# Grouping the 64-row matmul pairs of two FFN blocks, moving attention work, and reordering the head of a linear-attention + GeGLU kernel

## Chip, cores, metric

The kernel runs on one core of one Trainium2 chip. The metric is device time in microseconds (us): the median of several executions. "Span" is the time from the first to the last instruction of one profiled execution; it is about 1.7 us shorter than the time of the same execution.

## The reference

A block with two parallel branches on the same normalised input, B=1, S=2048, D=576, 32 heads of 18, F=4608, bf16:

```python
x  = A_x
xn = layernorm(x)
# A: linear attention.  phi(t) = where(t > 0, t + 1, exp(t)) + 1e-6
q, k, v = split_heads(xn @ wqkv)
kv = phi(k).T @ v ; z = sum_s phi(k)            # per head
o  = (phi(q) @ kv) / (phi(q) @ z + 1e-6)
# B: GeGLU
ffn = (gelu(xn @ w_gate) * (xn @ w_up)) @ w_down
return x + o @ wo + ffn
```

## The kernel before

The contraction length 576 is 4 x 128 + 64. The last 64 rows of `w_gate` and of `w_up` are put together in one 128-row tile `wr`, and the last 64 columns of xn are written twice (rows 0-63 and 64-127 of `xnT[:, 4]`). So the two short matmuls, one for gate and one for up, sit in different halves of the array and run at the same time; they are called a *pair* below. The kernel has this order:

1. Head. Per tile of 128 tokens: layernorm (statistics on VectorE, `rstd` on ScalarE), five transposes on TensorE, a copy of the result to `xnT` on VectorE, then K and V projections (20 matmuls of 288 columns). The kv sums accumulate two tiles behind.
2. Query projections.
3. Four chunks of 512 tokens. Each has a gate/up stage (36 column blocks of 128 features) and a down stage (4 tiles x 2 halves, 41 matmuls each).

```python
    load_x(0, 1)
    load_x(1, 1)
    load_wqkv_main(D, 2 * D)                                   # K
    nc.sync.dma_start(wqkv_sb[0:64, 4, :], A_wqkv[512:576, :]) # last 64 rows
    load_x(2, 2)                                               # a pair of x tiles
    load_wqkv_main(2 * D, 3 * D)                               # V
    load_wqkv_main(0, D)                                       # Q
    load_x(4, 4)
    ...
    def layernorm_transpose(n):
        ...
        for a_ in range(2):
            nc.vector.bn_stats(out=stats[:, a_, :], in_=xr[:, a_, :])
        ...                                                    # mv, rstd, xn
        for kt in range(KT):
            nc.tensor.transpose(tp[:, kt, :], xn[:, kt * P:(kt + 1) * P], ident[:])
        nc.vector.tensor_copy(out=xnT[:, :, n * P:(n + 1) * P], in_=tp[:, 0:KT, :])
    ...
    def gu_batch(sc, f0, r):
        wg, wu, wr, blk_dma = load_gu_block(f0, r)
        ...                                                    # 2r PSUM banks: g[i], u[i]
        for i in range(r):                                     # 8r matmuls, 128 rows
            for (pst, wsb) in ((g[i], wg), (u[i], wu)):
                for kt in range(4):
                    nc.tensor.matmul(pst[:], lhsT=wsb[:, kt, fcol], rhs=xnT[:, kt, cs], start=(kt == 0), stop=False)
        for i in range(r):                                     # r pairs, 64 rows
            nc.tensor.matmul(g[i][:], lhsT=wr[0:64, fcol], rhs=xnT[0:64, 4, cs], start=False, stop=True)
            nc.tensor.matmul(u[i][:], lhsT=wr[64:128, fcol], rhs=xnT[64:128, 4, cs], start=False, stop=True)
        for i in range(r):
            ...                                                # gelu on ScalarE, product on VectorE
    for sc in range(NSC):
        if sc == 0:
            for k in range(NF // 2):
                blk_dma = gu_batch(0, 2 * k, 2)
                if k >= NWBUF: load_wd_slice(after=blk_dma)
                if k < NS: attn_num(k)                         # attention of one tile
                if 1 <= k <= NS: attn_T(k - 1)
        else:
            for k in range(NF // RMAX):
                gu_batch(sc, RMAX * k, RMAX)                   # RMAX = 3
        for j in range(TPC):
            ...                                                # down projections
```

The order in which the instructions stand on each engine is not the order of this text: a scheduler decides it at build time from the dependencies and from a model of how long things take.

Of the kernel before, what the change touches and what calls it, by code (L numbers as in the profile page):

```python
# [8 lines left out]
ACT = mybir.ActivationFunctionType  # L9
ALU = mybir.AluOpType  # L10
BF16 = mybir.dt.bfloat16
F32 = mybir.dt.float32
PSUM = bass.MemoryType.PSUM

P = 128
S = 2048
D = 576
# [4 lines left out]
NS = S // P  # L22
NF = F // P
SC = 512
NSC = S // SC
TPC = SC // P
HALF = D // 2
DX = D + 64
KT = 5
# [7 lines left out]
EPS_ATT = 1e-6  # L37
RMAX = 3
NWBUF = 3
WDS = 2  # L40
NWARM = 36
KV_SKEW = 2

# [3 lines left out]
class _Ring:  # L47
    def __init__(self, tiles):
        self.tiles = tiles
        self.i = 0  # L50
# [8 lines left out]
def kernel(  # L59
# [12 lines left out]
    nc = tc.nc  # L72
# [3 lines left out]
    out_view = out_flat.rearrange("(n p) d -> p n d", p=P)  # L76
# [10 lines left out]
    def bank(name, *_):  # L87
        return psum.tile([P, 512], F32, name=name, tag="ps")
# [24 lines left out]
    def load_gu_block(f0, r):  # L113
        c0, c1 = f0 * P, (f0 + r) * P
        w = r * P
        wg = wg_bufs.next()
        wu = wu_bufs.next()
        wr = wr_bufs.next()
        nc.sync.dma_start(wg[:, :, :w], B_w_gate[0:512, c0:c1].rearrange("(kt p) c -> p kt c", p=P))
        nc.sync.dma_start(wu[:, :, :w], B_w_up[0:512, c0:c1].rearrange("(kt p) c -> p kt c", p=P))  # L120
        nc.sync.dma_start(wr[0:64, :w], B_w_gate[512:576, c0:c1])
        last = nc.sync.dma_start(wr[64:128, :w], B_w_up[512:576, c0:c1])
        return wg, wu, wr, last
# [9 lines left out]

    def load_x(n0, cnt):
        if cnt == 1:
            t = awork.tile([P, D], BF16, name="xs", tag="xs", bufs=2)
            nc.sync.dma_start(t[:], x_view[:, n0, :])
            x_src[n0] = t[:]
        else:
            t = awork.tile([P, 4, D], BF16, name="xg", tag="xg", bufs=2)  # L140
            nc.sync.dma_start(t[:, :cnt, :], x_view[:, n0:n0 + cnt, :])
            for i in range(cnt):
                x_src[n0 + i] = t[:, i, :]
# [4 lines left out]
    def load_wqkv_main(c0, c1):  # L148
        nc.sync.dma_start(wqkv_sb[:, 0:4, c0:c1], A_wqkv[0:512, c0:c1].rearrange("(kt p) c -> p kt c", p=P))

    load_x(0, 1)
    load_x(1, 1)
    load_wqkv_main(D, 2 * D)
    nc.sync.dma_start(wqkv_sb[0:64, 4, :], A_wqkv[512:576, :])
    load_x(2, 2)
    load_wqkv_main(2 * D, 3 * D)
    load_wqkv_main(0, D)
    load_x(4, 4)
    X_LATER = {3: (8, 4), 7: (12, 4)}

    bmask = const.tile([P, 7, DA], F32, name="bmask")
# [35 lines left out]
    def phi(ps_ap, out_ap, rows, cols, add_eng):  # L197
# [6 lines left out]
        )  # L204
        add_eng.tensor_tensor(out=out_ap, in0=e[:rows, :cols], in1=a[:rows, :cols], op=ALU.add)  # L205

    def layernorm_transpose(n):
        xt = x_src.pop(n)
        stats = asmall.tile([P, 2, nc.vector.BN_STATS_DIM], F32, name="stats")
        xr = xt.rearrange("p (a b) -> p a b", a=2)  # L210
        for a_ in range(2):
            nc.vector.bn_stats(out=stats[:, a_, :], in_=xr[:, a_, :])
        mv = asmall.tile([P, nc.vector.BN_AGGR_DIM], F32, name="mv")
        nc.vector.bn_aggr(out=mv[:], in_=stats[:])
        rstd = asmall.tile([P, 1], F32, name="rstd")
        nc.scalar.activation(out=rstd[:], in_=mv[:, 1:2], func=ACT.Ln, bias=eps_ln[:], scale=1.0)
        nc.scalar.activation(out=rstd[:], in_=rstd[:], func=ACT.Exp, scale=-0.5)
        xn = awork.tile([P, DX], BF16, name="xn")
        nc.vector.tensor_scalar(
            out=xn[:, 0:D], in0=xt, scalar1=mv[:, 0:1], scalar2=rstd[:],  # L220
            op0=ALU.subtract, op1=ALU.mult,
        )
        nc.vector.tensor_scalar(
            out=xn[:, D:DX], in0=xt[:, 512:D], scalar1=mv[:, 0:1], scalar2=rstd[:],
            op0=ALU.subtract, op1=ALU.mult,
        )
        tp = bank_bf16("tp_x", "tp", 1)
        for kt in range(KT):
            nc.tensor.transpose(tp[:, kt, :], xn[:, kt * P:(kt + 1) * P], ident[:])  # L229
        nc.vector.tensor_copy(out=xnT[:, :, n * P:(n + 1) * P], in_=tp[:, 0:KT, :])  # L230

    def kv_project(n):
        ts_ = slice(n * P, (n + 1) * P)
# [77 lines left out]
    def load_wd_slice(after=None):  # L311
        f0 = wd_loaded[0]
        if f0 < NF:
            d = nc.sync.dma_start(wd_sb[:, f0:f0 + WDS, :], wd_view[:, f0:f0 + WDS, :])
            if after is not None:
                tc.add_manual_dep(
                    d.ins, after.ins.name,
                    mybir.DependencyInfo(mybir.DependencyClass.NoSync, mybir.DependencyReason.DATA),
                    reason="w_down slice after the prefetched gate/up block on the same DMA queue",
                )  # L320
            wd_loaded[0] += WDS

# [27 lines left out]
    def attn_T(n):  # L350
        ts_ = slice(n * P, (n + 1) * P)
        o_sb = o_tiles.pop(n)
        tp = bank_bf16("tp_o")
        for kt, (r0, rn) in enumerate(OB):
            nc.tensor.transpose(tp[:rn, kt, :], o_sb[:, r0:r0 + rn], ident[:])  # L355
        nc.scalar.copy(out=oT[:, 0:3, ts_], in_=tp[:, 0:3, :])
        nc.scalar.copy(out=oT[:96, 3:5, ts_], in_=tp[:96, 3:5, :])

    def gu_batch(sc, f0, r):
        cs = slice(sc * SC, (sc + 1) * SC)  # L360
        wg, wu, wr, blk_dma = load_gu_block(f0, r)
        g = []
        u = []
        for i in range(r):
            g.append(bank("g"))
            u.append(bank("u"))
        for i in range(r):
            fcol = slice(i * P, (i + 1) * P)
            for (pst, wsb) in ((g[i], wg), (u[i], wu)):
                for kt in range(4):  # L370
                    nc.tensor.matmul(  # L371
                        pst[:], lhsT=wsb[:, kt, fcol], rhs=xnT[:, kt, cs],
                        start=(kt == 0), stop=False,
                    )
        for i in range(r):
            fcol = slice(i * P, (i + 1) * P)
            nc.tensor.matmul(g[i][:], lhsT=wr[0:64, fcol], rhs=xnT[0:64, 4, cs], start=False, stop=True)  # L377
            nc.tensor.matmul(u[i][:], lhsT=wr[64:128, fcol], rhs=xnT[64:128, 4, cs], start=False, stop=True)  # L378
        for i in range(r):
            gl = fwork.tile([P, SC], F32, name="gl")  # L380
            nc.scalar.activation(out=gl[:], in_=g[i][:], func=ACT.Gelu_apprx_tanh)  # L381
            nc.vector.tensor_tensor(out=hT[:, f0 + i, :], in0=u[i][:], in1=gl[:], op=ALU.mult)  # L382
        return blk_dma

    for sc in range(NSC):
        if sc == 0:
            nb = NF // 2
            for k in range(nb):
                blk_dma = gu_batch(0, 2 * k, 2)
                if k >= NWBUF:  # L390
                    load_wd_slice(after=blk_dma)
                if k < NS:
                    attn_num(k)
                if 1 <= k <= NS:
                    attn_T(k - 1)
            assert not o_tiles
            while wd_loaded[0] < NF:
                load_wd_slice()
        else:
            for k in range(NF // RMAX):  # L400
                gu_batch(sc, RMAX * k, RMAX)

        for j in range(TPC):
            n = sc * TPC + j
            ts_ = slice(n * P, (n + 1) * P)
            xres = fwork.tile([P, D], BF16, name="xres")
            nc.sync.dma_start(xres[:], x_view[:, n, :])
            res = fwork.tile([P, D], BF16, name="res")
            for hf in range(2):
                a_ps = bank("acc")  # L410
                for f in range(NF):
                    nc.tensor.matmul(  # L412
                        a_ps[:, :HALF], lhsT=hT[:, f, j * P:(j + 1) * P],
                        rhs=wd_sb[:, f, hf * HALF:(hf + 1) * HALF],
                        start=(f == 0), stop=False,
                    )
                for kt, (r0, rn) in enumerate(OB):
                    nc.tensor.matmul(  # L418
                        a_ps[:, :HALF], lhsT=oT[:rn, kt, ts_],
                        rhs=wo_sb[:rn, kt, hf * HALF:(hf + 1) * HALF],  # L420
                        start=False, stop=(kt == KT - 1),
                    )
                nc.vector.tensor_tensor(  # L423
                    out=res[:, hf * HALF:(hf + 1) * HALF], in0=a_ps[:, :HALF],
                    in1=xres[:, hf * HALF:(hf + 1) * HALF], op=ALU.add,
                )
            nc.sync.dma_start(out_view[:, n, :], res[:])


# [28 lines left out]
```

## Time and profile before

| | |
|---|---|
| time | 549.08 us, median of 6 runs (548.30 to 549.86) |
| profiled execution | 548.3 us, span 546.6 us |
| TensorE busy | 98% |
| first K matmul / query projections start | 11.07 / 60.61 us |
| gate/up of chunk 0, its down stage | 82.69, 40.22 us |
| gate/up of chunk 1, its down stage | 72.47, 40.22 us |

The rows with stages are differences between the first matmuls of the stages in the trace. These are lines of the page of the kernel before: busy time, the busy tenths of TensorE in 40 slices, the granted TensorE clock in the same slices, and the chain that ended last.

```profile
PE 535.4 (98%) x3495; PEld 313.7 (57%) x3528; DVE 193.6 (35%) x433; ACT 152.9 (28%) x346; POOL 44.6 (8%) x59
...
PE   5999999999999999999999999999999999999997
...
PEclk8999999999999999999999999999999999999999
...
PE 96%; DMA 1%; DVE 1%; issue 1%; SPq 0%; POOL 0%; ACT 0%; POOLq 0%; ACTq 0%
```

Only the first slice stands out. The Trainium skill ("Perfetto Trace Analysis", Identifying the Most-Contended Engine) warns that matmul busy time does not tell how near the engine is to its limit, because matmuls are pipelined. So look at starts, not at busy time. The timeline of TensorE over the head (start us, length us, engine, line, operation, count, idle before and what ended it):

```profile
5.57 1.27 PE L229 MATMUL tp_x<-ident,xn 128*128 128x128 bf16 x10
...
11.07 2.58 PE L239 MATMUL ps_k<-wqkv_sb,xnT 128*128 128x288 bf16 x10 [4.23 <-DVE xnT L230]
...
13.44 1.74 PE L248 MATMUL ps_v<-wqkv_sb,xnT 128*128 128x288 bf16 x10
...
15.02 0.44 PE L229 MATMUL tp_x<-ident,xn 128*128 128x128 bf16 x5
...
15.29 1.39 PE L239 MATMUL ps_k<-wqkv_sb,xnT 128*128 128x288 bf16 x10
```

The transposes of tiles 0 and 1 are done at 6.84 us, yet the first projection starts at 11.07: it waits for the copy of the transposed tile on VectorE. Ten K matmuls then take 2.58 us where the next tile's ten take 1.39. VectorE's timeline says why the copy was late:

```profile
8.09 1.18 DVE L212 BATCH_NORM_STATS2 stats<-xg 128x6 f32<-128x288 bf16 x3 [1.98 <-DMA xg<-in_A_x_dram]
...
10.53 0.88 DVE L230 COPY xnT<-tp_x 128x640 bf16<-128x640 bf16 x2
```

The statistics of x tiles 2 and 3 stand ahead of the copies of tiles 0 and 1 in VectorE's queue, and they waited for their load. The granted clock (the share of TensorE's full clock that it is given; 1.00 is full) fell in the gap (windows view, 11 to 15 us; after the five busy columns stand the granted clock, here 0.61, the DMA share and GB/s):

```profile
11.00:15.00 4.00, 3.93 (x20) 2.64 (x21) 3.01 (x11) 2.10 (x6) 1.06 (x2) 0.61 1.12 334
```

Inside a gate/up stage, the timeline of TensorE at the end of one block of three (last four 128-row matmuls, pairs, and the first four of the next block):

```profile
209.44 1.03 PE L371 MATMUL u<-xnT,wu 128*128 128x512 bf16 x4
210.40 0.39 PE L377 MATMUL g<-xnT,wr 64*128 64x512 bf16 x1
210.40 0.39 PE L378 MATMUL u<-xnT,wr 64*128 64x512 bf16 x1
...
210.84 0.38 PE L377 MATMUL g<-xnT,wr 64*128 64x512 bf16 x1
...
211.15 1.04 PE L371 MATMUL g<-xnT,wg 128*128 128x512 bf16 x4
```

Four matmuls of 512 columns at 216 ns each, start to start, should give way after 0.86 us; the first pair starts 0.96 us after 209.44. The last pair starts at 210.84 and the next 128-row matmul 0.31 us later, not 0.22. Each change of array mode (from 128-row to 64-row matmuls or back) loses almost 0.1 us, and no view calls TensorE's matmul side idle there. The side that loads weights (PEld) does show something; this is the start of another group of pairs:

```profile
222.47 0.09 PEld L377 LDWEIGHTS <-wr 64*128 64x128 bf16 x1 [0.42 <-issue]
```

The first weight load of the new mode starts 0.01 us before its matmul (222.48), where inside a mode it starts some 0.2 us ahead, and such a load takes 0.09 us, about what a change loses.

### The profile page before, as it was taken

The numbers are of one execution on the slowest core, as the hardware profiler recorded it, in microseconds if no ns is written. First come the engines' busy times: TensorE is split into PE (matmuls) and PEld (weight loads), VectorE is DVE, ScalarE is ACT, GpSimd is POOL, SyncE is SP. The second block draws the span as 40 slices with busy tenths as digits, with TensorE's granted clock in tenths as the row PEclk, the third lists the DMA queues.
The fourth block names the chain that finished last, engine by engine and source line by source line (L and its number), as shares of the span: only waits on it lengthen the run. The fifth ranks groups of instructions, "written<-read, shape, count | busy, mean of one in ns | idle before, by whom it ended". The sixth has DMA issues, their size and how long they took to land.

```text
span 546.6 us, 8832 instructions
## 1 busy us (share of the span) xinstructions
PE 535.4 (98%) x3495; PEld 313.7 (57%) x3528; DVE 193.6 (35%) x433; ACT 152.9 (28%) x346; POOL 44.6 (8%) x59
## 2 busy tenths in 40 slices
PE   5999999999999999999999999999999999999997
PEld 4888664444447774443467754444577644444775
DVE  6995597555541102322321112332301032233101
ACT  3887796333330002222310012322200022232000
POOL 1455463000000000000000000000000000000000
PEclk8999999999999999999999999999999999999999
DMA  9800004966762004544521024554401154440000
GB/s 282 248 2 2 1 2 122 271 194 194 193 199 82 27 23 124 158 131 135 169 87 43 23 88 132 160 164 130 131 23 42 41 169 140 131 130 1 23 12 22
DMA packets 79625, 58.08 MB, mean 106 GB/s; under 512 B 4448, under 2 KB 79520, under 8 KB 79584
## 3 DMA queue, kind: packets, MB, share of 16 engines
q1 hardware_dynamic: 79584, 57.53, 35.7%
q8 instruction: 27, 0.44, 0.3%
q14 instruction: 14, 0.11, 0.1%
HBM read 55.15 MB, written 2.36 MB: 105 GB/s over the span
## 4 chain that ended last, share of the span: by engine, by line
PE 96%; DMA 1%; DVE 1%; issue 1%; SPq 0%; POOL 0%; ACT 0%; POOLq 0%; ACTq 0%
PE acc L412 26%; PE g L371 23%; PE u L371 23%; PE g L377 7%; PE ps_q L294 4%; PE ps_k L239 4%; PE acc L418 4%; PE ps_v L248 3%; PE po L333 1%; DMA xg<-in_A_x_dram 1%; PE tp_o L355 1%; PE kv_ps L191 1%; PE tp_x L229 1%; DMA wr<-in_B_w_up_dram 0%; POOL pk L205 0%
## 5 line engine op out<-in xcount | busy, mean ns | idle before, releaser
L381 ACT ACTIVATE gl<-g 128x512 f32<-128x512 f32 x144 | 76.2, 596 | 330.4 <-PE u L378 330.3
L382 DVE TENSOR_TENSOR hT<-u,gl 128x512 bf16<-128x512 f32 x144 | 91.1, 684 | 190.6 <-ACT gl L381 190.6
L371 PE MATMUL u<-xnT,wu 128*128 128x512 bf16 x567 | 147.3, 379 | 0.8
L412 PE MATMUL acc<-wd_sb,hT 128*128 128x288 bf16 x1152 | 146.4, 286 | 0.0
L371 PE MATMUL g<-xnT,wg 128*128 128x512 bf16 x552 | 144.8, 380 | 1.0
L412 PEld LDWEIGHTS <-hT 128*128 128x128 bf16 x1152 | 112.2, 98 | 30.2 <-issue 1.7
L371 PEld LDWEIGHTS <-wu 128*128 128x128 bf16 x576 | 56.3, 98 | 68.0
L371 PEld LDWEIGHTS <-wg 128*128 128x128 bf16 x576 | 52.9, 98 | 69.7 <-issue 14.0
L423 DVE TENSOR_TENSOR res<-acc,xres 128x288 bf16<-128x288 f32 x32 | 14.6, 458 | 140.5 <-PE acc L418 140.5
L377 PE MATMUL g<-xnT,wr 64*128 64x512 bf16 x144 | 40.3, 380 | 0.0
L378 PE MATMUL u<-xnT,wr 64*128 64x512 bf16 x144 | 40.3, 380 | 0.0
L205 POOL TENSOR_TENSOR pk<-phi_e,phi_a 128x288 bf16<-128x288 f32 x32 | 25.1, 797 | 32.5 <-DVE phi_a L202 21.2
L239 PE MATMUL ps_k<-wqkv_sb,xnT 128*128 128x288 bf16 x160 | 23.4, 296 | 4.2 <-DVE xnT L230 4.2
L200 ACT ACTIVATE phi_e<-phi_e 128x288 f32<-128x288 f32 (+2 forms) x52 | 26.7, 514 | 1.5
L377 PEld LDWEIGHTS <-wr 64*128 64x128 bf16 x144 | 9.4, 94 | 27.1 <-issue 22.0
L418 PE MATMUL acc<-wo_sb,oT 128*128 128x288 bf16 (+1 forms) x160 | 24.9, 286 | 0.0
L248 PE MATMUL ps_v<-wqkv_sb,xnT 128*128 128x288 bf16 x160 | 22.6, 289 | 0.0
L294 PE MATMUL ps_q<-xnT,wqkv_sb 128*126 128x512 bf16 (+1 forms) x100 | 21.8, 379 | 0.0
L239 PEld LDWEIGHTS <-xnT 128*128 128x128 bf16 x160 | 15.4, 101 | 8.2 <-DVE xnT L230 4.5
L205 POOL TENSOR_TENSOR pqT<-phi_e,phi_a 126x512 bf16<-126x512 f32 (+1 forms) x14 | 17.5, 1270 | 10.9 <-ACT phi_e L200 5.2
L248 PEld LDWEIGHTS <-xnT 128*128 128x128 bf16 x160 | 15.9, 99 | 4.3
L418 PEld LDWEIGHTS <-oT 128*128 128x128 bf16 (+1 forms) x160 | 15.7, 98 | 3.9
(48 smaller groups left out, 242.0 us busy)
## 6 DMA issues: line engine op xcount, KB each, us to landing
wg<-in_B_w_gate_dram SPq DMA_DIRECT2D x36, 384.0 KB, 3.4
wu<-in_B_w_up_dram SPq DMA_DIRECT2D x36, 384.0 KB, 4.1
wd_sb<-in_B_w_down_dram SPq DMA_DIRECT2D x18, 288.0 KB, 3.3
wg<-in_B_w_gate_dram SPq DMA_DIRECT2D x18, 256.0 KB, 3.0
wu<-in_B_w_up_dram SPq DMA_DIRECT2D x18, 256.0 KB, 3.4
xres<-in_A_x_dram SPq DMA_DIRECT2D x16, 144.0 KB, 2.3
out_dram<-res SPq DMA_DIRECT2D x16, 144.0 KB, 1.8
wqkv_sb<-in_A_wqkv_dram SPq DMA_DIRECT2D x3, 576.0 KB, 6.2
```

Source lines behind the costliest of these rows:

```text
L200: nc.scalar.activation(out=e[:rows, :cols], in_=e[:rows, :cols], func=ACT.Exp, scale=-1.0)
L205: add_eng.tensor_tensor(out=out_ap, in0=e[:rows, :cols], in1=a[:rows, :cols], op=ALU.add)
L239: nc.tensor.matmul(ps_k[:, :HALF], lhsT=xnT[:, kt, ts_], rhs=wqkv_sb[:, kt, D + hf * HALF: D + (hf + 1) * HALF], start=(kt == 0), stop=(kt ...
L248: nc.tensor.matmul(ps_v[:, :HALF], lhsT=xnT[:, kt, ts_], rhs=wqkv_sb[:, kt, 2 * D + hf * HALF: 2 * D + (hf + 1) * HALF], start=(kt == 0), ...
L294: nc.tensor.matmul(ps[:rows, :], lhsT=wqkv_sb[:, kt, q0:q0 + rows], rhs=xnT[:, kt, sc * SC:(sc + 1) * SC], start=(kt == 0), stop=(kt == KT ...
L371: nc.tensor.matmul(pst[:], lhsT=wsb[:, kt, fcol], rhs=xnT[:, kt, cs], start=(kt == 0), stop=False,)
L377: nc.tensor.matmul(g[i][:], lhsT=wr[0:64, fcol], rhs=xnT[0:64, 4, cs], start=False, stop=True)
L378: nc.tensor.matmul(u[i][:], lhsT=wr[64:128, fcol], rhs=xnT[64:128, 4, cs], start=False, stop=True)
L381: nc.scalar.activation(out=gl[:], in_=g[i][:], func=ACT.Gelu_apprx_tanh)
L382: nc.vector.tensor_tensor(out=hT[:, f0 + i, :], in0=u[i][:], in1=gl[:], op=ALU.mult)
L412: nc.tensor.matmul(a_ps[:, :HALF], lhsT=hT[:, f, j * P:(j + 1) * P], rhs=wd_sb[:, f, hf * HALF:(hf + 1) * HALF], start=(f == 0), stop=False,)
L418: nc.tensor.matmul(a_ps[:, :HALF], lhsT=oT[:rn, kt, ts_], rhs=wo_sb[:rn, kt, hf * HALF:(hf + 1) * HALF], start=False, stop=(kt == KT - 1),)
```

## The change

Its intent: fewer changes of mode (two blocks of two put their pairs side by side: full, pairs | pairs, full; a change to the pairs and back is called a round trip), attention moved from the first gate/up stage to its down stage so that the eight PSUM banks are free for the doubled blocks, and an earlier start at the head. `w_down` is also loaded in 12 slices and not 18 (`WDS`), and each store of a result is split in two. Cut to its core:

```diff
-WDS = 2
+WDS = 3
-            t = awork.tile([P, D], BF16, name="xs", tag="xs", bufs=2)
+            t = awork.tile([P, D], BF16, name="xs", tag="xs", bufs=4)
...
-    load_wqkv_main(D, 2 * D)
-    nc.sync.dma_start(wqkv_sb[0:64, 4, :], A_wqkv[512:576, :])
-    load_x(2, 2)
-    load_wqkv_main(2 * D, 3 * D)
+    load_wqkv_main(D, D + HALF)
+    nc.sync.dma_start(wqkv_sb[0:64, 4, D:3 * D], A_wqkv[512:576, D:3 * D])
+    load_wqkv_main(D + HALF, 2 * D)
+    load_x(2, 1)
+    load_x(3, 1)
+    load_wqkv_main(2 * D, 2 * D + HALF)
+    load_wqkv_main(2 * D + HALF, 3 * D)
+    load_x(4, 4)
     load_wqkv_main(0, D)
-    load_x(4, 4)
+    nc.sync.dma_start(wqkv_sb[0:64, 4, 0:D], A_wqkv[512:576, 0:D])
...
-            nc.vector.bn_stats(out=stats[:, a_, :], in_=xr[:, a_, :])
+            st = nc.vector.bn_stats(out=stats[:, a_, :], in_=xr[:, a_, :])
+            if 2 <= n < 8:
+                tc.add_manual_dep(st.ins, xnT_copy[max(1, n - 2)].ins.name, ...)   # order on VectorE
...
+    def gu_double_batch(sc, f0, r):
+        a = _GuBatch(sc, f0, r)
+        a.alloc(); a.full(True);  a.pairs(False); a.geglu()
+        b = _GuBatch(sc, f0 + r, r)
+        b.alloc(); b.pairs(True); b.full(False);  b.geglu()
+        return a.blk_dma, b.blk_dma
...
         if sc == 0:
+            blks = [gu_batch(0, 0, 2)]
+            for k in range((NF - 4) // 4):
+                blks.extend(gu_double_batch(0, 2 + 4 * k, 2))
+                ...                                            # w_down slices, one per block
+            attn_num(0); attn_num(1)
+            blks.append(gu_batch(0, NF - 2, 2))
+            attn_T(0); attn_T(1)
         else:
-            for k in range(NF // RMAX):
-                gu_batch(sc, RMAX * k, RMAX)
+            for k in range(NF // 4):
+                gu_double_batch(sc, 4 * k, 2)
...
             for hf in range(2):
+                if sc == 0:
+                    grp = 2 * j + hf
+                    if grp >= 1: attn_T(2 * grp); attn_T(2 * grp + 1)
+                    if grp <= 6: attn_num(2 * grp + 2); attn_num(2 * grp + 3)
...
-            nc.sync.dma_start(out_view[:, n, :], res[:])
+                nc.sync.dma_start(out_view[:, n, hf * HALF:(hf + 1) * HALF], res[:, hf * HALF:(hf + 1) * HALF])
```

More of the change, by code (lines that the diff above doesn't have):

```diff
@@ L205, in phi @@
         add_eng.tensor_tensor(out=out_ap, in0=e[:rows, :cols], in1=a[:rows, :cols], op=ALU.add)
+    xnT_copy = {}
     def layernorm_transpose(n):
@@ L211, in layernorm_transpose @@
         for a_ in range(2):
-            nc.vector.bn_stats(out=stats[:, a_, :], in_=xr[:, a_, :])
+            st = nc.vector.bn_stats(out=stats[:, a_, :], in_=xr[:, a_, :])
+            if 2 <= n < 8:
+                tc.add_manual_dep(
+                    st.ins, xnT_copy[max(1, n - 2)].ins.name,
+                    mybir.DependencyInfo(mybir.DependencyClass.NoSync, mybir.DependencyReason.DATA),
+                    reason="VectorE copies earlier transposed tiles before it turns to an x tile that may still be in flight",
+                )
         mv = asmall.tile([P, nc.vector.BN_AGGR_DIM], F32, name="mv")
@@ L229, in layernorm_transpose @@
             nc.tensor.transpose(tp[:, kt, :], xn[:, kt * P:(kt + 1) * P], ident[:])
-        nc.vector.tensor_copy(out=xnT[:, :, n * P:(n + 1) * P], in_=tp[:, 0:KT, :])
+        xnT_copy[n] = nc.vector.tensor_copy(out=xnT[:, :, n * P:(n + 1) * P], in_=tp[:, 0:KT, :])
     def kv_project(n):
@@ L357, in attn_T @@
         nc.scalar.copy(out=oT[:96, 3:5, ts_], in_=tp[:96, 3:5, :])
-    def gu_batch(sc, f0, r):
-        cs = slice(sc * SC, (sc + 1) * SC)
-        wg, wu, wr, blk_dma = load_gu_block(f0, r)
-        g = []
-        u = []
-        for i in range(r):
-            g.append(bank("g"))
-            u.append(bank("u"))
-        for i in range(r):
-            fcol = slice(i * P, (i + 1) * P)
-            for (pst, wsb) in ((g[i], wg), (u[i], wu)):
-                for kt in range(4):
-                    nc.tensor.matmul(
-                        pst[:], lhsT=wsb[:, kt, fcol], rhs=xnT[:, kt, cs],
-                        start=(kt == 0), stop=False,
-                    )
-        for i in range(r):
-            fcol = slice(i * P, (i + 1) * P)
-            nc.tensor.matmul(g[i][:], lhsT=wr[0:64, fcol], rhs=xnT[0:64, 4, cs], start=False, stop=True)
-            nc.tensor.matmul(u[i][:], lhsT=wr[64:128, fcol], rhs=xnT[64:128, 4, cs], start=False, stop=True)
-        for i in range(r):
-            gl = fwork.tile([P, SC], F32, name="gl")
-            nc.scalar.activation(out=gl[:], in_=g[i][:], func=ACT.Gelu_apprx_tanh)
-            nc.vector.tensor_tensor(out=hT[:, f0 + i, :], in0=u[i][:], in1=gl[:], op=ALU.mult)
-        return blk_dma
@@ new lines, with __init__, alloc, full @@
+    class _GuBatch:
+        def __init__(self, sc, f0, r):
+            self.cs = slice(sc * SC, (sc + 1) * SC)
+            self.f0, self.r = f0, r
+            self.wg, self.wu, self.wr, self.blk_dma = load_gu_block(f0, r)
+            self.g = []
+            self.u = []
+        def alloc(self):
+            for i in range(self.r):
+                self.g.append(bank("g"))
+                self.u.append(bank("u"))
+        def full(self, first):
+            for i in range(self.r):
+                fcol = slice(i * P, (i + 1) * P)
+                for (pst, wsb) in ((self.g[i], self.wg), (self.u[i], self.wu)):
+                    for kt in range(4):
+                        nc.tensor.matmul(
+                            pst[:], lhsT=wsb[:, kt, fcol], rhs=xnT[:, kt, self.cs],
+                            start=(first and kt == 0), stop=(not first and kt == 3),
+                        )
+        def pairs(self, first):
+            for i in range(self.r):
+                fcol = slice(i * P, (i + 1) * P)
+                nc.tensor.matmul(self.g[i][:], lhsT=self.wr[0:64, fcol], rhs=xnT[0:64, 4, self.cs],
+                                 start=first, stop=not first)
+                nc.tensor.matmul(self.u[i][:], lhsT=self.wr[64:128, fcol], rhs=xnT[64:128, 4, self.cs],
+                                 start=first, stop=not first)
+        def geglu(self):
+            for i in range(self.r):
+                gl = fwork.tile([P, SC], F32, name="gl")
+                nc.scalar.activation(out=gl[:], in_=self.g[i][:], func=ACT.Gelu_apprx_tanh)
+                nc.vector.tensor_tensor(out=hT[:, self.f0 + i, :], in0=self.u[i][:], in1=gl[:], op=ALU.mult)
@@ new lines, in gu_batch @@
+    def gu_batch(sc, f0, r):
+        b = _GuBatch(sc, f0, r)
+        b.alloc()
+        b.full(True)
+        b.pairs(False)
+        b.geglu()
+        return b.blk_dma
+    def gu_double_batch(sc, f0, r):
+        a = _GuBatch(sc, f0, r)
+        a.alloc()
+        a.full(True)
+        a.pairs(False)
+        a.geglu()
+        b = _GuBatch(sc, f0 + r, r)
+        b.alloc()
+        b.pairs(True)
+        b.full(False)
+        b.geglu()
+        return a.blk_dma, b.blk_dma
+    assert NS == 16 and TPC == 4
@@ L385 @@
     for sc in range(NSC):
         if sc == 0:
-            nb = NF // 2
-            for k in range(nb):
-                blk_dma = gu_batch(0, 2 * k, 2)
-                if k >= NWBUF:
-                    load_wd_slice(after=blk_dma)
-                if k < NS:
-                    attn_num(k)
-                if 1 <= k <= NS:
-                    attn_T(k - 1)
-            assert not o_tiles
+            blks = [gu_batch(0, 0, 2)]
+            for k in range((NF - 4) // 4):
+                blks.extend(gu_double_batch(0, 2 + 4 * k, 2))
+                while len(blks) > NWBUF:
+                    blks.pop(0)
+                    load_wd_slice(after=blks[NWBUF - 1])
@@ L397 @@
+            attn_num(0)
+            attn_num(1)
+            blks.append(gu_batch(0, NF - 2, 2))
+            attn_T(0)
+            attn_T(1)
             while wd_loaded[0] < NF:
-                load_wd_slice()
+                load_wd_slice(after=blks[-1])
         else:
-            for k in range(NF // RMAX):
-                gu_batch(sc, RMAX * k, RMAX)
+            for k in range(NF // 4):
+                gu_double_batch(sc, 4 * k, 2)
         for j in range(TPC):
@@ L409 @@
             for hf in range(2):
+                if sc == 0:
+                    grp = 2 * j + hf
+                    if grp >= 1:
+                        attn_T(2 * grp)
+                        attn_T(2 * grp + 1)
+                    if grp <= 6:
+                        attn_num(2 * grp + 2)
+                        attn_num(2 * grp + 3)
                 a_ps = bank("acc")
```

## The prediction

> **What bounds it now.** TensorE: busy 98% of the 546.6 us span (busy table), 96% of the chain of waits. VectorE is at 35%, DMA near 36%. Only time on TensorE's own queue counts: its idle time and what it loses between matmuls. Both are small, and the matmul work does not change.
>
> Idle: the timeline of the first 15 us shows the one real gap. TensorE finishes ten transposes at 6.84 us, then waits to 11.07 for VectorE's copy of the transposed x (4.23 us in the waits view). VectorE stood idle 1.98 us for the next x pair (landed 8.07), queued ahead of that copy. The granted clock is then 0.5 from about 10.7 to 14.1, so tile 0's 20 projection matmuls take 4.1 us, not 2.45. Tile 1 starts at 15.46.
>
> Between matmuls: start to start, a 128-row 512-column matmul takes 216 ns; from a 128-row to a 64-row one about 311, back 308. A round trip into the 64-row pairs loses about 0.19 us. This agrees with the Trainium skill, "TensorEngine Tiling (Array Packing)", Key Properties: "Changing tiling mode (not just tile) drains the TensorE".
>
> **What the change does.**
> 1. Round trips. Before: 18 blocks of two in the first chunk + 3x12 of three = 54. After (built instruction order): 10 + 3x9 = 37. 17 x 0.187 = **3.2 us** saved, all on the critical path.
> 2. Attention numerators and transposes move from the first gate/up stage to its down projections. They cost about 0.55 us a tile, pure streaming, with no switch of their own. Moved: **0**. The gate/up stage shrinks from 82 to about 72 us, its down stage grows by about 8.
> 3. Head. The copy no longer stands behind x tiles 2 and 3. It can end near 6.7 us; the first half of K should have landed by about 5 (all of K landed at 6.08). Tile 0 then runs at full clock, ending near 9.6. TensorE then waits about 1.5 us for tile 2's transposes (VectorE work in its built order). Tile 1 starts near 11.3: **4.1 us** saved (2.5 to 5).
> 4. The last store halves; 144 KB land in 1.4 to 1.7 us: **0.1 us**.
> 5. DMA: the first gate/up stage moves 976 KB per block of about 4.0 us while w_down lasts (244 GB/s), against 832 per 4.65. The head moved 390 GB/s with 1152-byte packets, about 340 with 512-byte ones, so it should hold. Prefetch in chunks 1 to 3 falls from about 12 to 8 us ahead, against landings of 3 to 4. **0**, with a tail of 1 to 2 us.
>
> Sum: 7.4 us, so about **541.8 us** (1.3% faster), range 539.8 to 544.2. Faster by over 2% 0.05, within 2% 0.94, slower 0.01: over 2% needs 11 us, which these terms don't hold.
>
> **What would show it.** (1) 37 groups of pairs, each still losing 0.19 us; a double block of four lasting about 7.95 us. (2) First-chunk down groups about 6.1 us (the last 5.6), no idle before transposes. (3) First K matmul near 6.8 us, clock 1.0 after 7 us, tile 1 near 11.3. (5) DMA share near 0.8 early in the first gate/up stage, no TensorE wait for weights.
>
> **What would make it wrong.** VectorE becoming the limit of the first tiles, so that the early start is handed back; the clock window falling otherwise; TensorE waiting for weights in the first chunk; a switch costing more where the pairs open an accumulation.

## The result

The changed kernel took 541.84 us (median of 8 runs, 541.49 to 543.39) beside 549.31 us for the kernel before (16 runs, those of the first measurement included). The ratio is 0.9867, interval 0.9853 to 0.9881: 1.3% faster, which is "within 2%".

The page of the changed kernel, the same lines as above:

```profile
PE 530.3 (98%) x3496; PEld 315.5 (58%) x3528; DVE 198.7 (37%) x433; ACT 159.6 (30%) x346; POOL 44.5 (8%) x59
...
PE   6999999999999999999999999999999999999997
...
PEclk9999999999999999999999999999999999999999
...
PE 95%; DMA 2%; SPq 1%; issue 1%; POOL 0%; DVE 0%; ACT 0%; POOLq 0%; ACTq 0%
```

The busy share is still 98%. The head, on TensorE:

```profile
5.74 1.05 PE L241 MATMUL tp_x<-ident,xn 128*128 128x128 bf16 x10
7.04 1.40 PE L251 MATMUL ps_k<-wqkv_sb,xnT 128*128 128x288 bf16 x10 [0.25 <-DVE xnT L242]
9.46 1.61 PE L260 MATMUL ps_v<-wqkv_sb,xnT 128*128 128x288 bf16 x10 [1.01 <-DMA wqkv_sb<-in_A_wqkv_dram]
12.13 0.45 PE L241 MATMUL tp_x<-ident,xn 128*128 128x128 bf16 x5 [1.06 <-DVE xn L231]
12.42 1.39 PE L251 MATMUL ps_k<-wqkv_sb,xnT 128*128 128x288 bf16 x10
```

The 4.23 us wait is gone and the ten K matmuls take 1.40 us. Two smaller waits have come in its place: 1.01 us for the first half of V (landed 9.42), and 1.06 us for tile 2's normalised x. VectorE's timeline shows the copies ahead of tile 2's statistics now, and what the normalisation waited for; ScalarE's shows why:

```profile
6.50 0.89 DVE L242 COPY xnT<-tp_x 128x640 bf16<-128x640 bf16 x2
7.77 1.18 DVE L218 BATCH_NORM_STATS2 stats<-xs 128x6 f32<-128x288 bf16 x3 [0.38 <-DMA xs<-in_A_x_dram]
...
11.64 0.43 DVE L231 TENSOR_SCALAR xn<-xs,mv,rstd 128x576 bf16<-128x576 bf16 x1 [1.29 <-ACT rstd L229]
```

```profile
11.11 0.40 ACT L265 CAST v<-ps_v 128x288 bf16<-128x288 f32 x1 [0.24 <-PE ps_v L260]
11.40 0.21 ACT L229 ACTIVATE rstd<-rstd 128x1 f32<-128x1 f32 x1
```

The last step of `rstd` stands behind the copy of V's second half, which waits for V's second half to be computed, which waited for its weights (landed 10.25). So the load of V sets both waits. The clock from 11 to 15 us is full (the 1.00 before the last two columns):

```profile
11.00:15.00 4.00, 2.94 (x29) 2.38 (x29) 3.31 (x10) 2.59 (x9) 0.46 (x2) 1.00 1.09 323
```

Inside a gate/up stage, TensorE over the pairs of a double block:

```profile
211.33 1.03 PE L390 MATMUL u<-xnT,wu 128*128 128x512 bf16 x4
212.29 0.39 PE L398 MATMUL g<-xnT,wr 64*128 64x512 bf16 x1
...
212.94 0.38 PE L398 MATMUL g<-xnT,wr 64*128 64x512 bf16 x1
...
213.26 1.04 PE L390 MATMUL g<-xnT,wg 128*128 128x512 bf16 x4
```

Four pairs lie together between one change in (0.96 us) and one change out (0.32 us). The cost of a change is what it was; there are fewer. Stage by stage, from the first matmuls of the stages (the second profiles of both kernels come from later runs, told of below):

| us | before | before, 2nd profile | after | after, 2nd profile |
|---|---|---|---|---|
| query projections start | 60.61 | 61.35 | 57.76 | 57.32 |
| query projections | 21.60 | 21.60 | 21.61 | 21.60 |
| chunk 0, gate/up + down | 122.91 | 122.91 | 121.39 | 121.39 |
| chunk 1 | 112.69 | 112.69 | 112.05 | 112.06 |
| chunk 2 | 112.69 | 112.69 | 112.06 | 112.05 |
| chunk 3, gate/up | 72.47 | 72.47 | 71.85 | 71.85 |
| last down stage to the end | 43.59 | 43.60 | 43.59 | 43.60 |
| span | 546.56 | 547.31 | 540.31 | 539.87 |

Between the two profiles first at hand, 6.25 us went: 2.85 at the head and 3.41 in the stages. The medians differ by 7.5, and the difference needed an explanation as well: the stages repeat to 0.01 us, so it had to be the head.

### The profile page after: what moved, and what is told of

It is laid out like the page before. It is cut to its first block, busy times and chain, and to the rows that moved or that the text cites. A ratio compares the mean times of both kernels' runs of the same rounds, so it can differ in the third digit from the quotient of the medians.

```text
span 540.3 us, 9015 instructions
## 1 busy us (share of the span) xinstructions
PE 530.3 (98%) x3496; PEld 315.5 (58%) x3528; DVE 198.7 (37%) x433; ACT 159.6 (30%) x346; POOL 44.5 (8%) x59
## 4 chain that ended last, share of the span: by engine, by line
PE 95%; DMA 2%; SPq 1%; issue 1%; POOL 0%; DVE 0%; ACT 0%; POOLq 0%; ACTq 0%
PE acc L467 26%; PE g L390 23%; PE u L390 23%; PE g L398 6%; PE ps_q L306 4%; PE acc L473 4%; PE ps_v L260 3%; PE ps_k L251 3%; DMA wqkv_sb<-in_A_wqkv_dram 1%; DMA wg<-in_B_w_gate_dram 1%; PE tp_o L367 1%; PE po L345 1%; PE tp_x L241 1%; PE kv_ps L195 1%; SPq L137 0%
## 5 line engine op out<-in xcount | busy, mean ns | idle before, releaser
L406 ACT ACTIVATE gl<-g 128x512 f32<-128x512 f32 x144 | 82.0, 596 | 285.9 <-PE u L400 227.6
L407 DVE TENSOR_TENSOR hT<-u,gl 128x512 bf16<-128x512 f32 x144 | 96.1, 689 | 187.8 <-PE u L400 118.9
L398 PE MATMUL g<-xnT,wr 64*128 64x512 bf16 x144 | 37.4, 379 | 0.4
L400 PE MATMUL u<-xnT,wr 64*128 64x512 bf16 x144 | 37.4, 379 | 0.0
L209 POOL TENSOR_TENSOR pk<-phi_e,phi_a 128x288 bf16<-128x288 f32 x32 | 25.0, 795 | 29.7 <-DVE mv L226 11.3
L398 PEld LDWEIGHTS <-wr 64*128 64x128 bf16 x144 | 10.7, 94 | 24.0 <-issue 15.7
L251 PE MATMUL ps_k<-wqkv_sb,xnT 128*128 128x288 bf16 x160 | 22.2, 286 | 0.3 <-DVE xnT L242 0.3
L260 PEld LDWEIGHTS <-xnT 128*128 128x128 bf16 x160 | 15.6, 98 | 5.4 <-issue 1.5
L306 PEld LDWEIGHTS <-wqkv_sb 128*126 128x126 bf16 (+1 forms) x100 | 13.1, 131 | 8.3
```

What stands on the lines that cost most here:

```text
L209: add_eng.tensor_tensor(out=out_ap, in0=e[:rows, :cols], in1=a[:rows, :cols], op=ALU.add)
L251: nc.tensor.matmul(ps_k[:, :HALF], lhsT=xnT[:, kt, ts_], rhs=wqkv_sb[:, kt, D + hf * HALF: D + (hf + 1) * HALF], start=(kt == 0), stop=(kt ...
L260: nc.tensor.matmul(ps_v[:, :HALF], lhsT=xnT[:, kt, ts_], rhs=wqkv_sb[:, kt, 2 * D + hf * HALF: 2 * D + (hf + 1) * HALF], start=(kt == 0), ...
L306: nc.tensor.matmul(ps[:rows, :], lhsT=wqkv_sb[:, kt, q0:q0 + rows], rhs=xnT[:, kt, sc * SC:(sc + 1) * SC], start=(kt == 0), stop=(kt == KT ...
L398: nc.tensor.matmul(self.g[i][:], lhsT=self.wr[0:64, fcol], rhs=xnT[0:64, 4, self.cs], start=first, stop=not first)
L400: nc.tensor.matmul(self.u[i][:], lhsT=self.wr[64:128, fcol], rhs=xnT[64:128, 4, self.cs], start=first, stop=not first)
```

## The experiments

The theory at the start: head and round trips add, and nothing else in the change matters. The rivals: (a) the gain in the stages comes from smaller blocks and eight banks in turn, not from fewer round trips; (b) moving attention is worth something of its own; (c) the head gains by its load order, not by the order on VectorE; (d) the clock, and not the wait, is the head's loss. e1, e2, e3 and e6 ran together on one chip and shared runs of the kernel before; so did e4, e5, e7 and e8 on a second chip, and e9, b2 and after_again on a third. before_again ran later, on the first chip.

### One part alone (e1_head_only, e2_ffn_only)

```diff
# e1: the kernel before, with the load order, bufs=4 for the single x tiles, and the manual dependency of the change
# e2: the changed kernel, with these three undone
```

> The kernel before with the head of the change alone (load order, four single x tiles, the order given to VectorE). Sum theory, that head and round trips add: the profile shows the first projection matmul near 7.0 us, tile 1 near 12.4, the query projections starting 2.85 us earlier than before (60.61 to 57.8) and nothing else moved, so a span near 543.7 and a time 2.9 us under before. Clock theory, that the idle gap of before costs more in other executions than in the profiled one because the clock window falls differently: the time is about 4 us under before, and the runs of this kernel spread less (under 2 us) than those of before (548.3 to 551.5). Rival, that the head gain is handed back because VectorE limits the first tiles: under 1.5 us.

> The changed kernel with the head of the kernel before. Sum theory: head as before (query projections at 60.6 us), then 1.5 us saved in chunk 0 and 0.6 in each of chunks 1 to 3, together 3.4 us under before, span near 543.2. Clock theory: the runs spread as those of before do (about 3 us), since the idle gap is still there. Rival, that doubling only pays together with the earlier start: under 2 us.

Measured: e1 545.31 us (544.92 to 546.86) and e2 545.16 us (544.46 to 547.35), both beside 549.41 (11 runs); ratios 0.9928 (0.9914 to 0.9943) and 0.9923 (0.9907 to 0.9939). In e1's profile the query projections start at 57.49 and every stage after has the length of before (chunk 0: 122.91). In e2's they start at 61.45 and every stage has the length of the changed kernel (121.39, 112.06, 112.06, 71.84). So the two parts don't touch each other: the stages give 3.4 us, the head the rest. The two medians add up to 8.35 us where the change gives 7.5, which is inside the intervals. In size the sum theory missed: e1 is 4.1 us under before and not 2.9, with a spread of 1.9 us, as the clock theory had it, and e2 is 4.25 under and not 3.4. The second profiles below take this up.

### The pairs apart again (e3_pairs_apart)

```diff
         b.alloc()
-        b.pairs(True)
-        b.full(False)
+        b.full(True)
+        b.pairs(False)
         b.geglu()
```

> The changed kernel with the second block of each double block in the old order, full matmuls first and pairs last: same batches of two, same loads, same banks, but 72 round trips into the 64-row pairs and not 37. Round-trip theory: 35 x 0.187 us = 6.5 us slower than the changed kernel, so near 548.4 us; a double block lasts about 8.15 us and not 7.97. Rival, that the gain came from smaller batches and eight banks in turn: within 1 us of the changed kernel, near 542.

Measured: 548.98 us (548.76 to 549.19), ratio to before 0.9989 (0.9977 to 1.0001): the whole gain of the change is lost, though the head is as early as ever (query projections at 57.20). Chunk 0 takes 123.07 us, chunk 1 113.95 and chunk 3's gate/up 73.73, each longer than in the changed kernel; with chunk 2 that comes to 1.68 + 3 x 1.89 = 7.35 us for 35 more round trips, 0.21 us each. Rival (a) falls: batches, banks and loads are those of the changed kernel. The engines' line in the page of this run, and that of e7 (told of next), which has 37 groups of pairs as the changed kernel has:

```profile
PE 540.1 (99%) x3528; PEld 309.9 (57%) x3528; DVE 195.4 (36%) x433; ACT 155.8 (28%) x346; POOL 44.5 (8%) x59
...
PE 532.6 (99%) x3528; PEld 315.7 (58%) x3528; DVE 198.5 (37%) x433; ACT 159.6 (30%) x346; POOL 44.5 (8%) x59
```

e3's span is 7.2 us longer and its busy time 7.5 us: the lost time counts as busy. (The page of the changed kernel lacks 32 of the 3528 matmul records, so its 98% is a little too low to be set beside these.)

### Attention back (e7_attn_back)

```diff
             for k in range((NF - 4) // 4):
                 blks.extend(gu_double_batch(0, 2 + 4 * k, 2))
                 ...
-            attn_num(0)
-            attn_num(1)
+                if 2 * k < NS: attn_num(2 * k); attn_num(2 * k + 1)
+                if 1 <= k <= NS // 2 - 1: attn_T(2 * k - 2); attn_T(2 * k - 1)
             blks.append(gu_batch(0, NF - 2, 2))
-            attn_T(0)
-            attn_T(1)
+            attn_T(NS - 2); attn_T(NS - 1)
# and no attention in the down stage
```

> The changed kernel with the attention numerators and transposes back in the first gate/up stage, two tiles after each double block, and none in the down projections. Moved-only theory: same total, within 0.5 us of 541.9; gate/up of chunk 0 about 8.5 us longer and its down stage as much shorter. Rival, that the move is worth something of its own because attention takes PSUM banks out of the turn of eight and VectorE work between the blocks: TensorE waits for banks after the attention matmuls, 1 to 4 us slower.

Measured: 541.45 us (541.21 to 541.79), ratio to before 0.9849 (0.9837 to 0.9862). The gate/up stage of chunk 0 grows from 73.88 to 81.03 us, the down stage shrinks from 47.51 to 40.21: together 121.24 against 121.39. Rival (b) falls: the move is worth nothing, it even costs 0.15 us in these profiles. Attention was put elsewhere, not made cheaper. The reason given for the move, free PSUM banks, isn't borne out either: in e7's stages no TensorE wait is listed.

### Order on VectorE or order of loads (e4_head_no_order, e5_head_old_loads)

```diff
# e4: the changed kernel
-            if 2 <= n < 8:
-                tc.add_manual_dep(st.ins, xnT_copy[max(1, n - 2)].ins.name, ...)
# e5: the changed kernel, loads in the order of before, except
-    load_x(2, 2)
+    load_x(2, 1)
+    load_x(3, 1)
```

> The changed kernel without the order given to VectorE (the manual dependency of the statistics on earlier copies); the new load order stays. The built order then puts the statistics of tiles 2, 3, 4 and half of 5 ahead of the first copy. Order theory: the first copy waits for the group of tiles 4 to 7, which landed at 11.7 us in the changed kernel, so the first projection matmul starts near 14 us, behind even the kernel before (11.07), and the clock falls in the longer gap: 5 to 8 us slower than the changed kernel, 547 to 550. Load theory, that splitting and reordering the loads gives the head gain: within 1 us of 542.

> The changed kernel with the load order of the kernel before (x tiles 2 and 3 as two single loads, everything else as it was); the order given to VectorE stays. Order theory: first projection matmul near 7.4 us (when the last 64 rows of the weights have landed, 7.3 us before), V lands at about 9.6, tile 1 starts within 0.7 us of the changed kernel's 12.42, time within 0.7 us of 541.9. Load theory: the head gain is lost, 3 us or more slower.

Measured, beside 549.94 us (11 runs): e4 548.95 us (547.88 to 549.25), ratio 0.9979 (0.9964 to 0.9994); e5 543.04 us (542.02 to 545.94), ratio 0.989 (0.9867 to 0.9914). In e4 (VectorE's timeline, then TensorE's):

```profile
11.56 1.18 DVE L216 BATCH_NORM_STATS2 stats<-xg 128x6 f32<-128x288 bf16 x3 [1.12 <-DMA xg<-in_A_x_dram]
...
13.45 0.87 DVE L234 COPY xnT<-tp_x 128x640 bf16<-128x640 bf16 x2
```

```profile
13.98 2.58 PE L243 MATMUL ps_k<-wqkv_sb,xnT 128*128 128x288 bf16 x10 [7.30 <-DVE xnT L234]
```

The new loads alone make the head worse than before: the built order now puts even tiles 4 and 5 ahead of the first copy, and the wait grows from 4.23 to 7.30 us. In e5 (TensorE):

```profile
10.30 1.39 PE L257 MATMUL ps_v<-wqkv_sb,xnT 128*128 128x288 bf16 x10 [1.15 <-DMA wqkv_sb<-in_A_wqkv_dram]
12.74 0.45 PE L238 MATMUL tp_x<-ident,xn 128*128 128x128 bf16 x5 [1.06 <-DVE xn L228]
13.03 1.39 PE L248 MATMUL ps_k<-wqkv_sb,xnT 128*128 128x288 bf16 x10
```

With the old loads and the new order, tile 1 starts at 13.03 against 12.42. Three of six runs took 542.0 to 542.5 us; the others, 543.6, 545.8 and 545.9, had a mean granted clock of 0.996, 0.993 and 0.993 and not 0.999 to 1.000, and they made the median 1.2 us more than the changed kernel's (the intervals of the ratios overlap between 0.9867 and 0.9881). So rival (c) falls for the most part: the one manual dependency is the head's gain, and the loads add roughly 0.5 to 1 us to it. The dependency with x tiles 2 and 3 still loaded as a pair was not run.

### The clock (e6_gap_filled, e9_less_warm)

```diff
# e6: the kernel before, with 56 matmuls of the identity after the transposes of tiles 0 and 1
+        if n == 0:
+            fill = bank("fill")
+            for _ in range(56):
+                nc.tensor.matmul(fill[:, 0:P], lhsT=ident[:], rhs=ident[:], start=True, stop=True)
         pending.append(kv_project(n))
# e9: the changed kernel
-NWARM = 36
+NWARM = 20
```

> The kernel before with 56 more 128-column matmuls on the identity in TensorE's idle gap after the first ten transposes; they feed nothing. Clock theory: TensorE still waits for the copy until about 11.1 us, but the granted clock stays 1.0, so tile 0 takes 2.5 us and not 4.1: about 1.6 us under before in the profile, and if the gap costs more in other executions 2 to 2.7 us in the times, with a spread under 2 us. Wait theory, that only the wait counts and the clock does not: same time as before within 0.5 us, same spread.

> The changed kernel with 20 warm-up matmuls and not 36; the built order of all other instructions is the same, and TensorE has nothing else to do before 5.6 us. Clock theory, that half-speed windows at the head cost real time: the clock rises one or two windows of 3.4 us later than in the changed kernel (6.4 us), tile 0's 20 projection matmuls run at half speed, and the run is 0.7 to 2.5 us slower. Rival, that TensorE's waits at the head hide the clock: within 0.3 us of the changed kernel.

e6 took 552.58 us (551.69 to 553.04), 0.5% slower than before (ratio 1.0052, 1.004 to 1.0064), against both expectations. Tile 0 did run at full speed (its 20 matmuls took 2.5 us from 11.36), but the filling moved the scheduler's built order on VectorE and ScalarE, and at tile 1 this wait came in:

```profile
18.68 1.16 PE L249 MATMUL ps_v<-wqkv_sb,xnT 128*128 128x288 bf16 x5 [2.58 <-DVE phi_a L203]
```

So e6 changed two things and tells nothing of what the clock costs. e9 takes away 16 of the 36 matmuls on the identity with which both kernels open and whose results nothing uses; it was chosen because the built order of VectorE, ScalarE and the DMA queue stays the same. It took 541.95 us (541.43 to 542.11), beside 541.63 (541.46 to 543.60) for the changed kernel in the same rounds (after_again, below). TensorE in e9, and the start of tile 1 in after_again:

```profile
6.66 2.58 PE L251 MATMUL ps_k<-wqkv_sb,xnT 128*128 128x288 bf16 x10
9.03 2.08 PE L260 MATMUL ps_v<-wqkv_sb,xnT 128*128 128x288 bf16 x10
12.17 0.45 PE L241 MATMUL tp_x<-ident,xn 128*128 128x128 bf16 x5 [1.06 <-DVE xn L231]
```

```profile
11.98 1.39 PE L251 MATMUL ps_k<-wqkv_sb,xnT 128*128 128x288 bf16 x10
```

Tile 0 is at half speed here (2.58 us for ten, not 1.40), and the slow matmuls fill time in which TensorE would have waited for V. Tile 1 starts at 12.46, where it did in the first profile of the changed kernel (12.42), but 0.48 us later than in after_again, though V had landed earlier (8.68 and 9.64 us, there 8.99 and 9.81). So half speed in tile 0 costs the new head 0.3 us (medians) to 0.5 us (profiles), between what the two theories said. Half speed elsewhere seems to cost more. Of the 13 runs of the changed kernel on record, ten with a mean granted clock of 0.999 or 1.000 took 541.46 to 542.04 us and three with 0.996 took 543.30 to 543.60; by estimate that is one more half-speed window of 3.413 us, which is 0.003 of the span. No trace of one of these three was kept, so where the window lay stays open. In the old head tile 1 follows tile 0 without a wait, so there the half speed (about 4.1 us for tile 0 and not 2.5) should count in full; that is argued from the timeline, not shown by a run.

### Why the medians differ by more than the first profiles (before_again, after_again)

> The kernel before once more, for a second profile of it. Its runs have a median of 549.3 to 549.9 us, but the profiled one took 548.3, the fastest of all. Landing theory, from the run with the old head, whose pair of x tiles landed at 8.87 us and not at 8.07 and whose first projection matmul came exactly as much later (11.87 and not 11.07): the pair lands near 8.9 us, the first projection matmul near 11.9, the query projections near 61.4 and not 60.6, tile 0 takes the same 4.2 us, span near 547.5. Clock theory: the pair lands near 8.1 and the extra time lies in matmuls at half speed after 14.1 us, so that tile 1 or 2 take over 3 us.

> The changed kernel unaltered, on the same chip and in the same rounds as the two runs beside it, so that they can be compared: 541.5 to 543.5 us.

before_again, the unaltered kernel before, took 549.32 us (548.83 to 549.71); after_again, the unaltered changed kernel, 541.63 (ratio to before 0.986, 0.9841 to 0.9878). VectorE's line, then TensorE's, of before_again:

```profile
8.69 1.18 DVE L212 BATCH_NORM_STATS2 stats<-xg 128x6 f32<-128x288 bf16 x3 [2.54 <-DMA xg<-in_A_x_dram]
```

```profile
11.67 2.58 PE L239 MATMUL ps_k<-wqkv_sb,xnT 128*128 128x288 bf16 x10 [5.21 <-DVE xnT L230]
```

The pair of x tiles landed at 8.67 us and not at 8.07, and the first projection came 0.60 us later, at 11.67 and not at 11.07; the queries start 0.74 us later. e2, which has the same head, shows it again: landed 8.87, first projection 11.87, queries 61.45. The first profile of before was taken of the fastest of its runs. Against this second one the account closes: 61.35 - 57.32 = 4.03 us at the head, 3.41 in the stages, 7.44 of span (547.31 - 539.87), as the medians have it. For these two profiles the landing theory holds: it gives 0.60 of the 0.74 us, and tile 0, which takes 4.37 us here and 4.22 there, gives the rest; tiles 1 and 2 don't take the 3 us or more of the clock theory. The two second profiles come from two chips, and slower runs of before (550.9 us at a granted clock of 0.991) have no trace. The old head passed on whatever its loads did; in the new one the copy no longer waits for x tiles 2 and 3.

### How much room the weight loads have (e8_two_buffers)

```diff
-NWBUF = 3
+NWBUF = 2
```

> The changed kernel with two weight buffers and not three, so the prefetch of a gate/up block starts one block (about 4 us) ahead of its use and not two (8 us). If the DMA term is zero with a margin, this eats the margin: four issues of about 0.45 us and landings of 2.5 to 3.3 us come to 4 to 5 us, so TensorE waits up to 1 us a block, 10 to 60 us slower in all. If DMA were slack even at 4 us, no change.

Measured: 544.0 us (two runs), ratio 0.9895. The expectation was far off. TensorE waited for gate/up weights twice in the whole run, both in chunk 0, where `w_down` is loaded as well (waits view, window of chunk 0's gate/up; us in total, times, longest):

```profile
PE g L390 <- DMA wg<-in_B_w_gate_dram: 1.4, 1, 1.4
...
PE u L390 <- DMA wu<-in_B_w_up_dram: 0.7, 1, 0.7
```

Chunk 0 took 123.73 us and not 121.39; chunks 1 to 3 were as long as with three buffers. So the shorter prefetch of the change is safe by a wide margin.

### An attempt at a better one (b2_tuned_head)

```diff
# attention back as in e7; nine double blocks in chunk 0; and
     load_wqkv_main(2 * D, 2 * D + HALF)
+    load_x(2, 1)
     load_wqkv_main(2 * D + HALF, 3 * D)
+    load_x(3, 1)
# VectorE: statistics of tile 1 after tile 0's aggregation, of tile 3 after tile 2's normalisation
# ScalarE: tile 0's second V copy after tile 2's rstd
```

> An attempt to beat the changed kernel: attention back in the first gate/up stage, nine double blocks there (36 round trips in all, not 37), x tile 2 loaded between the halves of V and tile 3 after them, statistics of tile 1 after tile 0's aggregation and of tile 3 after tile 2's normalisation on VectorE, tile 2's rstd before tile 0's second V copy on ScalarE. If the two waits left at the head (1.0 us for V, 1.06 us for tile 2's normalisation) are what these orders cause, tile 1 starts near 11.2 us and not 12.4, and the time is 1 to 1.8 us under the changed kernel of the same rounds, near 540.5. If the loads themselves set the pace, under 0.5 us.

Measured: 543.49 us (543.12 to 543.75), ratio to before 0.9885 (0.987 to 0.99); the changed kernel took 541.63 in the same rounds. Tile 1 did start earlier, at 11.59 us against 11.98 in after_again, but the next wait came one tile on (TensorE's lines):

```profile
11.30 0.45 PE L253 MATMUL tp_x<-ident,xn 128*128 128x128 bf16 x5 [1.03 <-DVE xn L239]
...
15.45 0.45 PE L253 MATMUL tp_x<-ident,xn 128*128 128x128 bf16 x5 [1.25 <-DVE xn L239]
```

Putting tile 3's statistics behind tile 2's normalisation made tile 3 late, and the queries start at 58.93 and not at 57.32. The ninth double block didn't pay either: chunk 0 took 121.31 us, no less than e7's 121.24 with one round trip more, and a single matmul of its first double block came 0.29 us late. Of what was measured, nothing beats the changed kernel clearly. e7's stages are 0.15 us shorter and its median 0.4 us lower, but from other rounds.

## Why the prediction was right, point by point

- **The total.** 541.8 predicted, 541.84 measured; 1.3% and the class as predicted. Two of its terms were somewhat off in opposite directions, so the agreement to 0.04 us is luck; the range is what was earned.
- **Round trips, 3.2 us: right in mechanism, a little small in size.** There are 37 groups of pairs. e3 puts a round trip at 0.21 us, not 0.187: the two changes cost 95 and 92 ns, and the first matmuls in the new mode take about 10 ns more each. 17 x 0.21 is 3.6; the stages gave 3.41, and e7 shows 0.15 of the difference to be the moved attention. The drain on a change of mode that the Trainium skill states ("TensorEngine Tiling (Array Packing)", Key Properties) agrees with e3, which shows the cost of a change but not what the array does in it.
- **Moved attention, 0: right** (e7: 0.15 us the wrong way).
- **Head, 4.1 us: right in size against a typical execution, by a chain with one wrong link.** The first projection, which the first copy releases, started at 7.04 (6.54 in the second profile; 6.8 predicted). The failed step is "Tile 0 then runs at full clock, ending near 9.6": V's halves landed at 9.42 and 10.25, so tile 0 ended about 11.1 and tile 1 started at 12.42 (11.98 in the second profile), not 11.3. Step 3 has no term for the landing of V. What made up for it, by luck: the profile that the prediction started from was the luckiest run of before. Its tile 1 starts at 15.29 (15.46 in the prediction); in the second profile it is 16.04. The head's gain is 2.85 us between the first two profiles and 4.03 between the second two; e1's median has 4.1.
- **Last store, 0.1 us: not visible.** The last landing comes 1.61 us after its issue, not 1.73, but the last down stage to the end is 43.6 us in both kernels (and 43.3 in e2, 43.4 in e5, so this part varies more than the term).
- **DMA, 0: right.** TensorE waits for no weight load in the stages of the changed kernel; the DMA share in chunk 0's gate/up was 0.72 to 0.75 (0.8 predicted), and e8 shows that even half the prefetch would cost only 2.3 us there.
- **The clock: right as to what it would do** (full speed from 6.4 us). The page "TensorE: Matmul & The Clock Gate" (Trainium skill, Part 1) speaks of half speed in windows of 3413 ns; the clock records of before agree, one window of 3.413 us at 0.5 from 10.73 us, and two in before_again. What it is worth in the old head is left open (e6), as is where the slower runs of both kernels lose their time.

## What to carry to other kernels

When an engine is 98% busy, measure from start to start: a change of array mode is paid inside "busy" time, and grouping the work of one mode is worth the number of saved round trips times a cost that one line of the trace gives. When an engine's queue is in order, look at what stands ahead of the instruction that others wait for; one ordering dependency did here what new loads alone could not (they made it worse). And take a second profile before trusting a term of a few microseconds at the start of a kernel: first loads land differently from run to run.

## What the Trainium skill lacked or had wrong

- "TensorEngine Tiling (Array Packing)" says that a change of mode drains the array, but gives no cost. These runs: 0.21 us for a round trip from 128-row to 64-row matmuls and back (35 of them: 7.35 us).
- "TensorE: Matmul & The Clock Gate", Back-to-back issue gap, gives about 131 ns per matmul of 512 columns and 81 ns of 128 columns as what a real stream of weight loads and matmuls sustains. Here such streams ran at 216 ns (512 columns) and 56 ns (the transposes, 128 columns, and 56 matmuls in a row in e6), start to start, at full clock, which is what the same section gives for the isolated matmul.
- "DMA: Bandwidth & Descriptors", Specifications, has transfers from 512 bytes on at line rate. In the kernel before, packets of 512 bytes moved 345 GB/s (16.5 to 18.5 us) and those of 1152 bytes 390 (8 to 12 us). Elsewhere the page does give each packet a fixed overhead, and no run varies the packet size alone.
- No page says how much the landing of the first loads varies: in the same program, the first weight block landed at 6.08 us in one run and at 7.11 in another, and the x pair behind it at 8.07 and 8.67.
